# A fused attention and two-layer MoE kernel: the first softmax laid out anew on one Trainium2 core

## The chip, the core and the metric

The kernel runs on one NeuronCore of a Trainium2 chip. The metric is device time in microseconds, here the median of three runs. In the profile PE is TensorE (PEld its weight loads), DVE is VectorE, ACT is ScalarE, POOL is GpSimd, and SP is SyncE, which issues most DMAs.

## The reference, cut to what matters

```python
def mab(q, kv):                       # scale = 1 / sqrt(128)
    s = scale * (q @ kv.T)
    s = s - s.max(-1, keepdims=True)
    a = np.exp(s)
    a /= a.sum(-1, keepdims=True) + 1e-09
    return a @ kv
h = mab(inducing, x)                  # 32 x 128 queries against 12480 tokens: the first softmax
x = mab(x, h)                         # every token against the 32 rows of h: the second softmax
hid = x @ w_in                        # 128 -> 2048
x = (np.maximum(hid, 0) + alpha * np.minimum(hid, 0)) @ w_out     # 2048 -> 128
hid = x @ w_in2
out = (hid * np.cos(hid)) @ w_out2
```

The weights come as 64-bit floats, read as pairs of 32-bit words; the kernel puts fp32 values together from them.

## The kernel before, in words

x is 98 blocks of 128 tokens (the last two of 96). **The first softmax** goes through the blocks in units (UNITS, line 29: 8, 16, 16, 16, 16, 12, 8 and 4 blocks; unit 0 also takes the two short blocks). For a unit, TensorE transposes its blocks four at a time into PSUM (`transposes`, L199), and VectorE (L204) or ScalarE (L206) copies each four to SBUF. TensorE multiplies them with the 32 queries (`u_scores`, L218); VectorE takes the maximum over the unit's columns (L230) and spreads it over a masked tile mm4 (L232); TensorE sums that into the tile tm (`u_max`, L238), from which VectorE takes the running minimum nbias of the negated maxima (L240). ScalarE forms the exponentials with their row sums zpart, and the factor resc between the old and the new maximum (`u_exp`, L246, L250). VectorE turns the exponentials in 32x32 blocks (L248), TensorE multiplies them with x (`u_pv`, L262), and VectorE adds the product to the running sum hun (`u_sum`, L277) and the denominator to zt (`u_z`, L270). In the loop over units (lines 452 to 480) a unit's transposes stand in two halves, with the scores of the unit before, the exponentials of the one before that, and the products of the unit three back between them. mask4 is kept as a copy in PSUM (L189).

Between the unit's parts a planner, `fill` (line 316), puts **decode** steps: of each quarter of w_in and w_out VectorE takes the magnitude (L362), GpSimd clamps it (L370), ScalarE converts the lower word (L367), VectorE shifts (L374) and joins (L378), GpSimd adds (L382). The planner gives an engine's step only while the granted time (GRANTS) lasts. Nothing is reordered afterwards: every engine runs its instructions in the order of the program.

**After the softmax** tz (L498), the normalised ht (L505), then the product of ht with w_in (`w1_product`, L648), so that the second softmax's weights times w1s give the hidden layer. Tokens then go in tiles of 512. For tile T and slice f, L735 is the hidden product h from the tile's softmax weights a4, ScalarE's L758 its rounded high part, VectorE's L766 the low part, and L778 to L780 three products with the split w_out (tile 0 uses one whole-precision product, L776, two passes). Tiles 0, 1, 2 come first, eight slices of each. The second softmax of a chunk of tokens (`soft_exp`, `soft_norm`) ends with y_at (L575), a high part a_hi (L579) and a low part a_lo (L348, called from there), which SP's DMAs place as the tile's a4 (`load_a4`, L640); for tile 2 these are six loads. From about 155 us on the second layer runs along.

Loads: x comes in parts of 8 blocks on SP's queue, two of four blocks first, but blocks 8 to 15 on ScalarE's queue (line 161), and the words of the weights behind them.

## Time and profile before

| | |
|---|---|
| median of 3 runs | 969.64 us (968.85 to 970.51) |
| span of the profiled execution | 967.3 us |
| busy share of the span: PE, DVE, ACT, POOL | 99%, 84%, 84%, 74% |
| shares of the chain that ended last: PE, DVE | 93%, 3% |

The span is the time from the first to the last instruction of one execution; the profile gives no other time for that execution, and a run's time also holds what lies around its span. A row of the timeline gives start, duration, engine, line, operation, output and input; the brackets at its end are the idle time of the engine before it and what ended it.

### The profile page before, as it was taken

Reading aid. Unit: us, or ns where it says so; the run is one execution under the profiler, and the core shown is the slowest. Engines: PE = TensorE matmul, PEld = TensorE weight load, DVE = VectorE, ACT = ScalarE, POOL = GpSimd, SP = SyncE. Lnnn points to the kernel's source line nnn. Section 1 sums busy time; section 2 is a strip of 40 time slices with the busy share of each in tenths; the row PEclk is TensorE's granted clock in tenths of the full one; section 3 lists DMA queues with packets and bytes.
Section 4 is the critical chain, followed back from the end, with each engine's and each line's share of the span. In section 5 each row is a group of like instructions: output and inputs, shape, how many; then the busy total and the mean of one; then the engine's idle time right before and its main releaser. Section 6 shows DMA issues by size and latency. Waiting matters only on the chain.

```text
span 967.3 us, 14953 instructions
## 1 busy us (share of the span) xinstructions
PE 955.3 (99%) x4608; PEld 771.6 (80%) x4608; DVE 810.2 (84%) x1378; ACT 810.8 (84%) x1577; POOL 712.6 (74%) x698
## 2 busy tenths in 40 slices
PE   8899999999999999999999999999999999999998
PEld 5566778888888888888888888888888888888886
DVE  4886877888888888888988888898888888888888
ACT  4677877888888888888888888898888888888897
POOL 2265656477778777877887778788777777877896
PEclk9999999999999999999999999999999999999999
DMA  9320000000000000000000000000000000000000
GB/s 360 147 93 25 25 17 9 1 1 20 19 20 2 12 20 20 1 12 20 20 1 21 11 17 4 20 20 12 1 20 20 2 11 20 20 1 15 12 13 16
DMA packets 12143, 26.54 MB, mean 27 GB/s; under 512 B 2752, under 2 KB 3360, under 8 KB 12064
## 3 DMA queue, kind: packets, MB, share of 16 engines
q1 hardware_dynamic: 11520, 24.95, 7.5%
q8 instruction: 36, 0.59, 0.3%
q10 hardware_dynamic: 544, 0.65, 0.2%
q14 instruction: 43, 0.35, 0.1%
HBM read 14.80 MB, written 6.39 MB: 22 GB/s over the span
## 4 chain that ended last, share of the span: by engine, by line
PE 93%; DVE 3%; ACT 1%; DMA 1%; issue 1%; POOL 0%; SPq 0%; ACTq 0%; DVEq 0%; POOLq 0%
PE h L812 9%; PE h L813 9%; PE h L814 9%; PE yacc L875 9%; PE yacc L873 9%; PE h L735 9%; PE yacc L874 9%; PE xacc L780 8%; PE xacc L779 8%; PE xacc L778 8%; PE xacc L776 1%; PE s L218 1%; DMA xp<-x_main 1%; PE tp L199 1%; PE xacc L786 1%
## 5 line engine op out<-in xcount | busy, mean ns | idle before, releaser
L348 POOL TENSOR_TENSOR lo<-g,hi 128x512 fp32r<-128x512 f32 (+1 forms) x398 | 505.7, 1273 | 160.7 <-PE yacc L874 42.3
L827 DVE SCALAR_TENSOR_TENSOR r<-k,h 128x512 f32<-128x512 int32 (+1 forms) x400 | 268.8, 672 | 103.1 <-ACT k L821 95.2
L821 ACT ACTIVATE k<-h 128x512 int32<-128x512 f32 (+1 forms) x400 | 235.2, 588 | 100.2 <-PE h L814 87.3
L839 DVE SCALAR_TENSOR_TENSOR g<-r,h 128x512 f32<-128x512 f32 (+1 forms) x400 | 266.9, 667 | 3.2 <-ACT r L833 1.7
L766 DVE SCALAR_TENSOR_TENSOR lo<-h,hi 128x512 fp32r<-128x512 f32 (+1 forms) x371 | 246.6, 670 | 21.0 <-ACT hi L758 20.3
L833 ACT ACTIVATE r<-r 128x512 f32<-128x512 f32 (+1 forms) x400 | 246.9, 617 | 1.6 <-DVE r L827 1.6
L758 ACT ACTIVATE hi<-h 128x512 fp32r<-128x512 f32 (+1 forms) x371 | 214.9, 581 | 19.5 <-PE h L735 18.0
L735 PE MATMUL h<-a,w1s 128*128 128x512 f32 (+1 forms) x400 | 158.9, 401 | 1.3 <-DMA a<-a_hi 0.5
L875 PE MATMUL yacc<-lo,wo 128*128 128x512 f32 (+1 forms) x400 | 154.5, 386 | 0.4 <-POOL lo L348 0.4
L873 PE MATMUL yacc<-hi,wo 128*128 128x512 f32 (+1 forms) x400 | 154.6, 386 | 0.0
L874 PE MATMUL yacc<-hi,wo 128*128 128x512 f32 (+1 forms) x400 | 154.0, 385 | 0.0
L780 PE MATMUL xacc<-lo,wp 128*128 128x512 f32 (+1 forms) x384 | 148.2, 386 | 0.0
L779 PE MATMUL xacc<-hi,wp 128*128 128x512 f32 (+1 forms) x371 | 142.8, 385 | 0.0
L778 PE MATMUL xacc<-hi,wp 128*128 128x512 f32 (+1 forms) x371 | 142.4, 384 | 0.0
L859 ACT ACTIVATE hi<-g 128x512 fp32r<-128x512 f32 (+1 forms) x201 | 124.4, 619 | 1.2 <-DVE g L839 1.2
L863 POOL TENSOR_SCALAR hi<-g 128x512 fp32r<-128x512 f32 x189 | 117.5, 622 | 6.0 <-DVE g L839 6.0
L812 PE MATMUL h<-xr_xt,wi 128*128 128x512 f32 (+1 forms) x272 | 105.1, 386 | 0.3
L814 PE MATMUL h<-xr_xt,wi 128*128 128x512 f32 (+1 forms) x272 | 104.2, 383 | 0.0
L813 PE MATMUL h<-xr_xt,wi 128*128 128x512 f32 (+1 forms) x272 | 104.2, 383 | 0.0
L735 PEld LDWEIGHTS h<-a,w1s 128*128 128x128 f32 x400 | 75.2, 188 | 28.4 <-issue 5.4
L875 PEld LDWEIGHTS yacc<-lo,wo 128*128 128x128 f32 x400 | 75.2, 188 | 16.5 <-POOL lo L348 1.3
L873 PEld LDWEIGHTS yacc<-hi,wo 128*128 128x128 f32 x400 | 75.2, 188 | 14.8
(152 smaller groups left out, 1113.4 us busy)
## 6 DMA issues: line engine op xcount, KB each, us to landing
out<-y SPq DMA_DIRECT2D x24, 256.0 KB, 2.0
xp<-x_main SPq DMA_DIRECT2D x10, 512.0 KB, 8.2
raw_wi<-w_in SPq DMA_DIRECT2D x8, 512.0 KB, 9.2
raw_wo<-w_out SPq DMA_DIRECT2D x8, 512.0 KB, 9.0
a<-a_hi SPq DMA_DIRECT2D x40, 64.0 KB, 2.0
a<-a_lo SPq DMA_DIRECT2D x20, 64.0 KB, 2.0
xp<-x_main SPq DMA_DIRECT2D x2, 256.0 KB, 3.5
xp<-x_main ACTq DMA_DIRECT2D x1, 512.0 KB, 7.1
```

Source lines behind the costliest of these rows:

```text
L348: eng.tensor_tensor(out=out, in0=in0, in1=in1, op=ALU.subtract)
L735: mm(t[:, :w], w1s[:, 128 * f:128 * f + 128], a4[T][:, :w], start=True, stop=True)
L766: dve.scalar_tensor_tensor(out=lo[:, :w], in0=t[:, :w], scalar=0.0, in1=hi[:, :w].bitcast(F32), op0=ALU.max, op1=ALU.subtract)
L779: mm(t[:, :w], wslice(wp, f, 1), hi[:, :w], start=False, stop=False)
L780: mm(t[:, :w], wslice(wp, f, 0), lo[:, :w], start=False, stop=False)
L821: act(out=k[:, :w], in_=h2s[T, f][:, :w], func=AF.Copy, bias=0.25)
L827: dve.scalar_tensor_tensor(out=r[:, :w], in0=k[:, :w], scalar=0.25, in1=h2s[T, f][:, :w], op0=ALU.subtract, op1=ALU.subtract)
L833: act(out=r[:, :w], in_=r[:, :w], func=AF.Sin, scale=-TWO_PI)
L839: dve.scalar_tensor_tensor(out=g[:, :w], in0=r[:, :w], scalar=TWO_PI, in1=h2s.pop((T, f))[:, :w], op0=ALU.mult, op1=ALU.mult)
L873: mm(t[:, :w], wslice(wo, f, 0), hi[:, :w], start=(f == 0), stop=False)
L874: mm(t[:, :w], wslice(wo, f, 1), hi[:, :w], start=False, stop=False)
L875: mm(t[:, :w], wslice(wo, f, 0), lo[:, :w], start=False, stop=(f == NF - 1))
```

## The change

1. Units of 8, 16, 16, 16, 16, 16 and 8 blocks: seven instead of eight. 2. All transposes of a unit in one run; nine of the groups of four are copied by VectorE, at other places than before. 3. `u_scores` is cut into products and `u_top` (maximum and mask multiply), `u_exp` into exponentials and `u_turn`; the loop's order is new. 4. Blocks 8 to 15 are loaded on SP's queue. 5. The denominator `u_z` goes to GpSimd. 6. mask4 is read in SBUF. 7. The planner's grants are new. 8. The second w1 product moves from before tile 0 into its steps. 9. `warm` (transposes whose result nobody reads) takes a PSUM tile of its own.

```diff
@@ -26,7 +26,7 @@
-UNITS = [(0, 8), (8, 16), (24, 16), (40, 16), (56, 16), (72, 12), (84, 8), (92, 4)]
+UNITS = [(0, 8), (8, 16), (24, 16), (40, 16), (56, 16), (72, 16), (88, 8)]
@@ -88,9 +88,8 @@
     NU = len(UNITS)
-    PV = 3
...
-    GRANTS = {2: (0.3, 0.1), 3: (0.45, 0.2), 4: (0.45, 0.2), 5: (0.45, 0.2)}
...
+    GRANTS = {3: (0.5, 0.25), 4: (0.5, 0.25), 5: (0.5, 0.25), 6: (0.5, 0.25)}
     ident = const.tile([128, 128], F32, name="ident")
@@ -158,7 +157,7 @@
     nc.scalar.dma_start(out=xp[12][0:96], in_=x_tail)
-    load_x(nc.scalar, 8, 8)
+    load_x(nc.sync, 8, 8)
     nc.scalar.dma_start(out=alph, in_=alpha)
@@ -185,8 +184,6 @@
     tmt = ps_tile("acc", "tm")
-    mask = tmt[:, 504:508]
-    dve.tensor_copy(out=mask, in_=mask4)
     tht, pv_last = tmt[:, 112:240], tmt[:, 240:368]
@@ -199,7 +196,7 @@
-        k = nb // 2 if b0 == 92 else nb if b0 in (0, 8, 24, 40) else 0
+        k = nb if b0 in (0, 12, 20, 28, 36, 48, 64, 80, 92) else 0
         if k:
@@ -207,8 +204,9 @@
+        t = ps_tile("h2", "warm")
         for _ in range(n):
-            nc.tensor.transpose(pvt[1][:, 384:512], ident, ident)
+            nc.tensor.transpose(t[:, 0:128], ident, ident)
@@ -227,9 +225,12 @@
         scores(t, o, indt, b0, nb, 4)
...
+    def u_top(n):
+        t = s1t[n]
         dve.reduce_max(out=mxu[:, n:n + 1], in_=t[:, 0:32 * len(unit_blocks(n))], axis=AX.X)
         mm4 = xpool.tile([128, 4], F32, tag="mm4", name="mm4", bufs=2)
-        dve.tensor_scalar(out=mm4, in0=mask4 if n == NU - 1 else mask, scalar1=mxu[:, n:n + 1], scalar2=None, op0=ALU.mult)
+        dve.tensor_scalar(out=mm4, in0=mask4, scalar1=mxu[:, n:n + 1], scalar2=None, op0=ALU.mult)
         s1t[n, "m"] = mm4
@@ -241,23 +242,26 @@
         w = 32 * len(unit_blocks(n))
-        p = xs[:, 5]
-        pt = ptt[n] = xs[:, n % 5]
+        p = xs[:, 4 + n % 2]
+        pt = ptt[n] = xs[:, n % 4]
         act(out=p[:, :w], in_=s1t.pop(n)[:, :w], func=AF.Exp, scale=scale, bias=nbias[:, n:n + 1],
             accum_out=zpart[:, n:n + 1])
-        dve.transpose(out=pt[:, :w], in_=p[:, :w])
         if n:
             act(out=resc[:, n:n + 1], in_=nbias[:, n - 1:n], func=AF.Exp, scale=-1.0, bias=nbias[:, n:n + 1])
+        s1t[n, "p"] = p
...
+    def u_turn(n):
+        w = 32 * len(unit_blocks(n))
+        dve.transpose(out=ptt[n][:, :w], in_=s1t.pop((n, "p"))[:, :w])
...
-    def u_pv(n, half):
+    def u_pv(n):
         bl = unit_blocks(n)
         r = pv_region(n)
-        h = len(bl) // 2
-        for k in range(h * half, h if half == 0 else len(bl)):
+        for k in range(len(bl)):
             g = k % 4
@@ -265,10 +269,10 @@
         if n == 0:
-            dve.tensor_copy(out=z, in_=zpart[:, 0:1])
+            pool.tensor_copy(out=z, in_=zpart[:, 0:1])
         else:
-            dve.scalar_tensor_tensor(out=z, in0=z, scalar=resc[:, n:n + 1], in1=zpart[:, n:n + 1],
-                                     op0=ALU.mult, op1=ALU.add)
+            pool.tensor_scalar(out=z, in0=z, scalar1=resc[:, n:n + 1], scalar2=zpart[:, n:n + 1],
+                               op0=ALU.mult, op1=ALU.add)
@@ -451,56 +455,51 @@
         b0, nb = UNITS[n]
-        quads = [(b0 + k, 4) for k in range(0, nb, 4)]
         gd, ga = GRANTS.get(n, (0.0, 0.0))
-        for k in quads[:max(1, len(quads) // 2)]:
-            transposes(*k)
+        for k in range(0, nb, 4):
+            transposes(b0 + k, 4)
         if n == 0:
             transposes(96, 2, 96)
+        fill(1.9, dve=gd, act=ga)
+        if n >= 4:
+            u_sum(n - 4)
+        if n >= 2:
+            u_max(n - 2)
         if n >= 1:
...
             u_exp(n - 2)
-        fill(1.8, dve=2 * gd, act=2 * ga)
-        if n >= PV:
-            u_pv(n - PV, 0)
-            u_pv(n - PV, 1)
-        if n == NU - 1:
-            u_scores(n)
-        for k in quads[max(1, len(quads) // 2):]:
-            transposes(*k)
+            u_z(n - 2)
+            u_turn(n - 2)
+        if n >= 3:
+            u_pv(n - 3)
         if n >= 1:
-            u_max(n - 1)
-        if n >= PV:
-            u_z(n - PV)
-            u_sum(n - PV)
+            u_top(n - 1)
         if n == 2:
             dve.tensor_scalar(out=om_a, in0=alph, scalar1=-1.0, scalar2=1.0, op0=ALU.mult, op1=ALU.add)
-        if n < NU - 1:
-            fill(1.8, dve=2 * gd, act=2 * ga)
-    u_pv(NU - 3, 0)
-    u_pv(NU - 3, 1)
+        fill(2.1, dve=gd, act=ga)
+    u_max(NU - 2)
+    u_scores(NU - 1)
+    u_exp(NU - 2)
+    u_z(NU - 2)
+    u_sum(NU - 4)
+    u_pv(NU - 3)
+    u_top(NU - 1)
+    u_turn(NU - 2)
     u_max(NU - 1)
-    u_exp(NU - 2)
     u_exp(NU - 1)
-    warm(3)
-    u_pv(NU - 2, 0)
-    u_pv(NU - 2, 1)
-    u_z(NU - 3)
+    u_z(NU - 1)
+    u_pv(NU - 2)
     u_sum(NU - 3)
-    u_z(NU - 2)
-    warm(2)
-    u_pv(NU - 1, 0)
-    u_pv(NU - 1, 1)
...
-    u_z(NU - 1)
+    u_turn(NU - 1)
     tz = ps_tile("h2", "tz")[:, 0:32]
     mm(tz, zt.to_broadcast([128, 128]), id32, start=True, stop=True)
+    u_pv(NU - 1)
     u_sum(NU - 2)
...
     dve.reciprocal(out=zr, in_=zr)
-    warm(3)
+    warm(2)
     mm(tht, hun, ssum2, start=True, stop=True)
@@ -671,7 +670,6 @@
     run(e1, 1)
-    w1p1 = w1_product(1)
     act(out=w1s[0:96, 0:512], in_=w1p[0:96, :], func=AF.Copy)
@@ -679,9 +677,7 @@
     run(e1, 2)
-    act(out=w1s[0:96, 512:1024], in_=w1p1[0:96, :], func=AF.Copy)
     run(e1, 3, 4)
-    w1_low(1, w1p1)
     plan(("soft", 2), "soft", then(soft_exp(2), soft_norm(2)), first=True)
@@ -928,7 +924,7 @@
         soon = steps[s + 2][0] if s + 2 < S else None
-        if soon and soon[0] == 0 and soon[1] in (8, 12):
+        if soon and soon[0] == 0 and soon[1] in (4, 8, 12):
             w1_parts(soon[1] // 4, w1_product(soon[1] // 4))
```

Where the order moves, as the built programs have it. First **VectorE, one unit in the middle of the softmax**, before (mm is the masked tile, tm holds the sums of maxima, xs the exponentials, s the scores in PSUM, k_t and g_ab decode's steps):

```order
L230 TENSOR_REDUCE mxu<-s_349 128x1
L232 TENSOR_SCALAR mm_355<-tm,mxu 128x4
L248 STREAM_TRANSPOSE xs<-xs 128x512
L240 TENSOR_REDUCE nbias<-tm 128x1
L270 SCALAR_TENSOR_TENSOR zt<-zt,resc,zpart 128x1
L277 SCALAR_TENSOR_TENSOR hun<-hun,resc,pv_161 128x128
L362 TENSOR_SCALAR g_ab<-raw_wi_131 128x512
```

and now:

```order
L279 COPY hun<-pv_160 128x128
L241 TENSOR_REDUCE nbias<-tm 128x1
L255 STREAM_TRANSPOSE xs<-xs 128x512
L231 TENSOR_REDUCE mxu<-s_359 128x1
L233 TENSOR_SCALAR mm_385<-mask_67,mxu 128x4
L378 TENSOR_SCALAR k_t_294<-g_ab 128x512
L201 COPY xt_89<-tp 128x512
L382 SCALAR_TENSOR_TENSOR k_t_294<-raw_wo_123,k_t_294 128x512
```

The turn stood ahead of the minimum nbias and belonged to the unit before; now it stands right behind the minimum, and belongs to the same unit. The denominator step zt has gone to GpSimd; there it stands ahead of decode's clamps and adds:

```order
L274 TENSOR_SCALAR zt<-zt,resc,zpart 128x1
L374 TENSOR_SCALAR g_ab<-g_ab 128x512 x2
L274 TENSOR_SCALAR zt<-zt,resc,zpart 128x1
L386 TENSOR_TENSOR win_86<-k_t_291,win_86 128x512
L274 TENSOR_SCALAR zt<-zt,resc,zpart 128x1
L386 TENSOR_TENSOR wout_87<-k_t_294,wout_87 128x512
```

Before, the same clamps and adds followed each other there with nothing between them. Third, **VectorE from decode to the a_lo of tile 2**, before (wa belongs to the folded weights, sT and rz to the second softmax, h_801 is the first product of tile 1):

```order
L560 RECIPROCAL rz_80<-rz_80 128x8
L571 TENSOR_TENSOR sT<-sT,rz_80 128x256
L696 TENSOR_TENSOR wa<-twt,alph 128x128
L575 STREAM_TRANSPOSE y_at<-sT 128x256
L542 STREAM_TRANSPOSE sT<-s_750 128x512
L545 TENSOR_REDUCE mx_79<-sT 128x16
L766 SCALAR_TENSOR_TENSOR lo_805<-h_801,hi_804 128x512
L348 TENSOR_TENSOR a_lo<-y_at,a_hi 128x256
```

and now (h_767 is the first product of tile 1):

```order
L762 SCALAR_TENSOR_TENSOR lo_771<-h_767,hi_770 128x512
L557 TENSOR_REDUCE rz_80<-sT 128x8
L558 TENSOR_SCALAR rz_80<-rz_80 128x8
L559 RECIPROCAL rz_80<-rz_80 128x8
L570 TENSOR_TENSOR sT<-sT,rz_80 128x256
L762 SCALAR_TENSOR_TENSOR lo_788<-h_784,hi_787 128x512
L574 STREAM_TRANSPOSE y_at<-sT 128x256
L762 SCALAR_TENSOR_TENSOR lo_797<-h_793,hi_796 128x512
L762 SCALAR_TENSOR_TENSOR lo_808<-h_801,hi_807 128x512
L352 TENSOR_TENSOR a_lo<-y_at,a_hi 128x256
```

The denominator, the division and the turn of chunk 2 have moved behind the first low part of tile 1, and a_lo behind the fourth.

## Rows read from the trace of the kernel before

**Rows 1.** Windows by stage: length, busy us of each engine (instructions), PEclk, DMA, GB/s
```profile
15.93:38.70 22.77, 21.31 (x371) 14.97 (x372) 20.10 (x58) 16.57 (x42) 6.27 (x7) 1.00 0.78 307
...
55.40:64.67 9.27, 9.27 (x39) 5.70 (x39) 5.95 (x11) 6.82 (x13) 5.80 (x7) 1.00 0.10 32
64.67:950.00 885.33, 884.13 (x3947) 722.95 (x3947) 753.01 (x1222) 759.76 (x1450) 678.70 (x646) 1.00 0.05 14
```
**Rows 2.** Timeline of TensorE: eight transposes early, products and eight transposes later
```profile
8.90 1.94 PE L199 MATMUL tp<-ident,xp 128*128 128x128 f32 x8 [2.21 <-DMA xp<-x_main]
...
26.86 1.06 PE L262 MATMUL pv<-xp,xs 128*32 128x128 f32 x32
27.85 1.09 PE L199 MATMUL tp<-ident,xp 128*128 128x128 f32 x8
```
**Rows 3.** DMA issues: count, KB each, median us from issue to landing
```profile
xp<-x_main SPq DMA_DIRECT2D x2, 256.0 KB, 3.5
```
**Rows 4.** Timeline of VectorE in one unit of the first softmax
```profile
24.23 0.68 DVE L230 TENSOR_REDUCE mxu<-s 128x1 f32<-128x512 f32 x1
24.95 0.22 DVE L232 TENSOR_SCALAR mm<-tm,mxu 128x4 f32<-128x4 f32 x1
25.08 0.70 DVE L248 STREAM_TRANSPOSE xs<-xs 128x512 f32<-128x512 f32 x1
...
25.88 0.34 DVE L277 SCALAR_TENSOR_TENSOR hun<-hun,resc,pv 128x128 f32<-128x128 f32 x1
26.14 0.42 DVE L362 TENSOR_SCALAR g_ab<-raw_wi 128x512 int32<-128x512 int32 x1
```
**Rows 5.** Timeline: exponential of 512 columns; minimum, exponential and turn of 256 columns
```profile
18.73 0.68 ACT L246 ACTIVATE xs<-s,nbias 128x512 f32<-128x512 f32 x1
...
35.21 0.18 DVE L240 TENSOR_REDUCE nbias<-tm 128x1 f32<-128x28 f32 x1
...
35.48 0.47 ACT L246 ACTIVATE xs<-s,nbias 128x256 f32<-128x256 f32 x1 [0.54 <-DVE nbias L240]
...
36.08 0.45 DVE L248 STREAM_TRANSPOSE xs<-xs 128x256 f32<-128x256 f32 x1
```
**Rows 6.** Timeline of VectorE: a copy of four blocks, decode's shift and join
```profile
14.47 0.69 DVE L204 COPY xt<-tp 128x512 f32<-128x512 f32 x1 [0.39 <-PE tp L199]
...
29.95 0.41 DVE L374 TENSOR_SCALAR k_t<-g_ab 128x512 int32<-128x512 int32 x1
30.40 0.69 DVE L378 SCALAR_TENSOR_TENSOR k_t<-raw_wi,k_t 128x512 int32<-128x512 int32 x1
```
**Rows 7.** Timeline: GpSimd adds, and a small VectorE operation beside one
```profile
24.45 1.27 POOL L382 TENSOR_TENSOR wout<-k_t,wout 128x512 int32<-128x512 int32 x1 [1.15 <-DVE k_t L378]
...
52.37 1.27 POOL L382 TENSOR_TENSOR win<-k_t,win 128x512 int32<-128x512 int32 x1 [0.16 <-DVE k_t L378]
52.59 1.08 DVE L559 TENSOR_SCALAR rz<-rz 128x8 f32<-128x8 f32 x1
```
**Rows 8.** Timeline of VectorE: first low part of tile 1, a_lo of tile 2
```profile
57.13 0.69 DVE L766 SCALAR_TENSOR_TENSOR lo<-h,hi 128x512 fp32r<-128x512 f32 x1 [0.90 <-ACT hi L758]
57.74 0.41 DVE L348 TENSOR_TENSOR a_lo<-y_at,a_hi 128x256 fp32r<-128x256 f32 x1
```
**Rows 9.** Timeline of SP, loads of tile 2: the second and the last; DMA issues
```profile
58.19 0.51 SPq L640 DMA_DIRECT2D a<-a_lo  x1
...
60.65 0.59 SPq L640 DMA_DIRECT2D a<-a_hi  x1
...
a<-a_hi SPq DMA_DIRECT2D x8, 32.0 KB, 1.8
```
**Rows 10.** Chain that ended last: a whole-precision pair, scores of 16 blocks, a split product
```profile
48.95 0.86 PE xacc L776 x2
...
57.96 1.00 PE s L218 x8
...
60.70 0.23 PE xacc L779
```

## The prediction

> **What bounds the kernel now.** I read the busy time by stage first [rows 1]. From 64.67 us (the first product of the third token tile) to 950 us TensorE is busy 884.13 of 885.33 us: nothing else can end anything there, so whatever the change moves before 64.67 us arrives at the end one for one. All of the diff's work lies before it. In the first softmax, 15.93 to 38.70 us, TensorE is busy 21.31 and VectorE 20.10 of 22.77 us: two engines close to full, and the question is which one the new layout makes the longer. From 55.40 to 64.67 us TensorE never idles; what it needs there must be on time.
>
> The profiled span is 967.3 us, the median of the three runs 969.64. I work out a difference on the span and add it to the median; the 2.3 us around the span stay.
>
> **1. Until the first full reduce.** Now TensorE waits 2.21 us for blocks 8 to 15, and the eight transposes after that wait take 1.94 us; at 27.85 eight take 1.09 [rows 2]. The load becomes the third on SP's queue, issued near 2.2 us. The two before it land 3.5 us after issue [rows 3], on ScalarE's queue it lands at 8.8; so 5.7 to 8.8, and I take 7.0. But the scores of unit 0 now stand behind sixteen transposes instead of four, and behind VectorE's third copy and its memset. Forward from 7.0: sixteen transposes 3.9 (at the slow rate; 2.2 at the fast one), last copy and memset 0.8, scores 1.3, sixteen transposes of unit 2 2.1, copy 0.7, and on VectorE the minimum, exponential and turn of unit 0, which now stand ahead of the reduce of unit 1, 1.6: 17.4; with fast transposes and scores 15.0. I take 16.5, nearer the slow end since the slow rate in [rows 2] lasts right up to there. It is 15.93 now [rows 1]: **+0.6** (-0.9 to +1.5).
>
> The Trainium skill (DMA: Bandwidth & Descriptors, section on issuing engines not being separate DMA queues) says that loads from either queue run on the same 16 engines and interleave, so that a second issuing engine saves only issue time. By that rule the move alone brings the load no sooner, and the total would be that of the fourth rival below; no run here shows it yet.
>
> **2. VectorE's chain per unit.** An instruction starts up to 0.1 us before the one ahead of it ends (turn at 25.08, multiply at 24.95 for 0.22). From start to start I take reduce 0.72, multiply 0.13, turn 0.63, sum 0.26, decode's magnitude 0.3 [rows 4], minimum 0.1 [rows 5], a 512-column copy 0.65, shift 0.45, join 0.61 [rows 6]. Now the order in a unit is reduce, multiply, turn of the unit before, minimum: the exponential that the turn needs was started by the previous minimum, and VectorE does not wait. In the new order the minimum of a unit is followed at once by its own turn. Between them stands ScalarE: exponential 0.27 us after the minimum's start, turn 0.60 after that for 256 columns, and 0.21 more for 512 (0.68 against 0.47) [rows 5]. So **1.08 us from a minimum to its turn, of which VectorE works 0.1**, five times, with everything behind it in its queue waiting too. TensorE gets the next products of maxima only after the multiply, and stalls behind them.
>
> To that come nine copies instead of four and a half (+4.5 x 0.65 = 2.9), less the eight denominator steps that go to GpSimd (0.1 each), one unit less (0.9) and 0.4 of decode.
>
> There is one price more. The multiply reads mask4 in SBUF instead of PSUM. An SBUF operation of that size, 128x8, took 1.08 us while a GpSimd add ran beside it, ending as that add ended; the multiply from PSUM took 0.22 at 24.95, inside the add at 24.45 to 25.72 [rows 4, 7]. In the new order the denominator steps stand ahead of decode's GpSimd steps and wait for the exponential, which pushes clamps and adds onto the multiplies of units 2, 3 and 4. I count 0.4, 0.5 and 0.45: 1.35 (0 if they miss one another, 3.0 if each meets an add whole).
>
> Reduce to reduce, with what the order puts between: unit 1 to 2, 0.72 + 0.13 + 0.13 (om_a) + 0.65 + 2 x 0.31 (magnitudes) + 1.08 + 0.63 = 3.96; 2 to 3, with the hold 0.4, shift and join 1.06 and the first sum 0.2, 4.87; 3 to 4, with 0.5, 1.06 and 0.26, 5.03; 4 to 5, with 0.45, 0.3 and 0.26, 4.22; from there to the minimum of the last unit 3.62 (0.85, decode 1.06, 1.08, 0.63); to the last sum about 2.15 (exponential 0.27 and 0.5, resc 0.3, GpSimd's denominator 0.2 and its product 0.3 ahead of the last eight products 0.5). Sum 23.85 us, against 22.77 from the full reduce to the last sum now [rows 1]: **+1.1** (-0.25 without any hold, +2.7 with all). TensorE's own work per 16-block unit is 2.1 transposes, about 0.9 scores and 1.0 products [rows 2, 10] and some 0.2 of maxima, 4.2, less than VectorE's 4.5, so it is not the bound.
>
> **3. Hand-over.** The second w1 product leaves the wait before the first tile and stands in another gap, before the transposes of the second tile's weights: nothing. With its copy and subtraction gone from ahead of that tile's exponential, VectorE is 0.5 us earlier there, but TensorE has the product itself, 0.86. Decode stands behind: wout's second quarter is only begun after the softmax, its scaled copy comes late for the fifth product of the first tile: **+0.2** (0 to +0.9).
>
> **4. Loads of the third tile.** The a_lo split for it now ends at 58.15, and the last of its six loads is issued at 60.65 and lands 1.8 later, 62.45 [rows 8, 9], 2.2 us before TensorE wants it at 64.67. In the new order VectorE has decode, then the third chunk's turn and maximum, then the first low part of tile 1, and only then denominator, division and turn of chunk 2 (0.41 + 0.17 + 0.2 + 0.43 + 0.43 at 256 columns, priced by the 0.41 of [rows 8]), with three more low parts at 0.61 among them, before a_lo: 57.13 + 4 x 0.61 + 1.64 = 61.2, and 0.41 for itself, 61.6. The loads follow as before, 4.3 us: 65.9. TensorE is there sooner: 8 products h and 12 split products at 0.23, 3 whole-precision pairs at 0.86, one set of scores 1.0 [rows 10] make 8.2 after 55.40, so 63.6. **+2.2 us** of idle TensorE, nothing behind it can pass (0 if the loads overlap better than now, +3.1 with one GpSimd hold).
>
> Equal units, one run of transposes and "three units late" by themselves cost nothing: the products already are three units late.
>
> **Sum**: 0.6 + 1.1 + 0.2 + 2.2 = 4.1: span 971.4, median **973.7 us**, +0.4%. A measurement of this kernel tells about 0.2% (1.94 us) from no change.
>
> **The rivals.**
> - *The loads are in time*: only the softmax term is left, 969.64 + 1.9 = 971.5. For: DMA issues could come earlier than VectorE's queue lets me think. Against: from the second issue to the last it takes 2.46 us in [rows 9], and a_lo is in front. Chance 0.17.
> - *TensorE slows down*: it would idle 1 to 2 us at several units and 2.2 at the loads. The transposes after the wait of 2.21 us run at half the later rate [rows 2], though the granted clock column reads 1.00 (2.4 GHz) for the stages of [rows 1]. Half rate for the last two units' products costs 1.5, after the loads 1 or more: 976.2. Against: the transposes before that wait were slow as well. The Trainium skill (TensorE: Matmul & The Clock Gate, part 1) states that an idle array falls to 1.2 GHz and activity brings back 2.4; by that rule this rival holds if the waits are long enough. Chance 0.12.
> - *TensorE, not VectorE, carries the softmax*, and it ends earlier. If VectorE's wait for the exponential were filled, a unit costs 4.2 and the stage ends with TensorE's own work: 72 transposes 9.2, scores 5.4, products 6.1, maxima 1.2 from the memset at 11.7, 33.6, and 2 of tail, 35.6 instead of 38.70. With terms 3 and 4 that is 968.9, no slower than before; with the loads in time 966.7, faster. It decides where VectorE's unit falls under 4.2. For: TensorE never waits for x. Against: the order puts turn right behind minimum. Chance 0.12.
> - *Blocks 8 to 15 still land at 8.8*: term 1 grows by 1.8, 975.5. For: all x loads share the traffic of the first 20 us, and this one gains only its place in a line. Against: the line ahead of it is two loads of 256 KB. Chance 0.06.
> - Something else, such as waits further on by a shifted order of decode, about no change: 0.04. The forecast keeps 0.49.
>
> **How the numbers follow.** Slower by over 0.2% (above 971.6) are nearly all of the forecast, the slow TensorE, the late blocks, and little of the first rival; faster (below 967.7) half of the third and a part of the unknown: 0.12 faster, 0.24 same, 0.64 slower. The range goes from the third rival's 968.9 to the second's 976.2; the forecast's own is 971.6 to 975.6.
>
> **What would show it.** Right: in the changed profile every turn of a unit has idle VectorE before it, ended by the exponential, about 1 us; TensorE waits for the mask multiply; the last sum starts near 40.4; a wait of TensorE of some 2 us for a_hi near 65. Wrong: no idle before the turns and a last sum before 38 (third rival); no DMA wait near 65 (first); transposes or products past 30 us at half rate (second).

## The result, and the profile after

The changed kernel takes **982.28 us** (median of four runs, 981.52 to 982.78) against 969.44 (968.85 to 970.51) for the kernel before, run beside it: ratio 1.0126, 95% interval 1.0114 to 1.0138. It is slower by 12.8 us. 973.7 had been predicted, in a range up to 976.2: the sign was right, the size three times too small.

Where the time went is read from windows whose edges are the same events in every kernel: start of the full reduce of unit 1, start of the last sum, and the starts of the first product h of tile 1, of tile 2, of tile 3 and of tile 8. First the profile after (columns as in [rows 1]):

```profile
0.00:18.26 18.26, 13.38 (x90) 10.18 (x91) 5.53 (x14) 5.35 (x10) 4.34 (x17) 0.81 0.90 336
18.26:41.96 23.70, 18.10 (x338) 12.45 (x336) 18.32 (x46) 12.38 (x32) 6.32 (x11) 1.00 0.67 257
41.96:48.62 6.66, 4.57 (x40) 2.95 (x40) 5.08 (x17) 2.75 (x8) 1.79 (x2) 1.00 0.01 2
48.62:60.13 11.51, 10.79 (x48) 5.14 (x49) 8.45 (x19) 8.64 (x19) 6.04 (x7) 1.00 0.19 51
60.13:71.87 11.74, 8.89 (x34) 4.81 (x35) 8.92 (x16) 7.74 (x15) 6.71 (x7) 1.00 0.21 65
71.87:113.00 41.13, 39.35 (x187) 25.96 (x188) 27.04 (x46) 30.74 (x60) 21.11 (x21) 1.00 0.14 43
113.00:201.37 88.37, 84.94 (x366) 66.83 (x367) 66.98 (x104) 66.09 (x120) 48.97 (x50) 0.98 0.04 11
```

The same windows of the kernel before, beside the two that stand in [rows 1]:

```profile
0.00:15.93 15.93, 11.65 (x74) 8.08 (x75) 3.86 (x11) 4.91 (x9) 4.13 (x16) 1.00 0.89 330
...
38.70:45.20 6.50, 5.66 (x46) 3.72 (x46) 5.04 (x17) 2.77 (x8) 1.13 (x2) 1.00 0.01 3
45.20:55.40 10.20, 9.47 (x46) 4.82 (x47) 9.32 (x22) 8.15 (x19) 5.66 (x6) 1.00 0.29 93
...
64.67:103.74 39.07, 38.59 (x186) 25.38 (x185) 30.06 (x50) 30.86 (x63) 21.05 (x22) 1.00 0.16 48
103.74:188.09 84.35, 83.73 (x367) 65.76 (x368) 65.53 (x104) 65.82 (x119) 49.47 (x51) 1.00 0.05 12
```

In lengths, with two kernels of the experiments (runs e10 and e9 below):

| stage | before | after | softmax of after, order of before | softmax of before, order of after |
|---|---|---|---|---|
| to the full reduce | 15.93 | 18.26 | 17.05 | 15.42 |
| to the last sum | 22.77 | 23.70 | 24.76 | 22.48 |
| to the first h | 6.50 | 6.66 | 6.44 | 6.50 |
| first half of tile 0 | 10.20 | 11.51 | 10.22 | 11.51 |
| first half of tile 1 | 9.27 | 11.74 | 9.25 | 11.73 |
| tile 2 to tile 3 | 39.07 | 41.13 | 39.54 | 42.76 |
| tile 3 to tile 8 | 84.35 | 88.37 | 84.41 | 88.20 |

After minus before: 2.33 + 0.93 + 0.16 = 3.42 up to the first h, then 1.31 + 2.47 + 2.06 + 4.02 = 9.86, of which the prediction had only term 4 and the 0.2 of term 3. The distance is 13.28 us at the start of tile 8 and 13.25 at the last product. These are single executions; how far the first row varies is said under term 1.

What TensorE waited for from 45 to 200 us (engine and line, releaser, us in total, times, longest), before:

```profile
PE tst L619 <- DVE y_st L348: 0.7, 1, 0.7
PE h L735 <- DMA a<-a_hi: 0.5, 1, 0.5
PE h L735 <- DVE lo L766: 0.4, 2, 0.2
```

and after:

```profile
PE h L731 <- DVE lo L762: 4.0, 5, 2.5
PE h L731 <- DMA a<-a_hi: 4.0, 2, 2.6
PE tst L618 <- DVE y_st L352: 1.4, 1, 1.4
PE xacc L772 <- ACT w1t L412: 0.4, 1, 0.4
```

The wait of 2.6 for a_hi is the one that term 4 priced. The longest for a low part, 2.5, lies in tile 6, nearly 130 us after the softmax. VectorE there, after:

```profile
164.09 0.69 DVE L800 TENSOR_TENSOR xr_xt<-xacc,xr_xt 128x512 fp32r<-128x512 f32 x1 [0.23 <-ACT xr_xt L799]
164.70 0.68 DVE L557 TENSOR_REDUCE rz<-sT 128x16 f32<-128x512 f32 x1
165.41 1.24 DVE L558 TENSOR_SCALAR rz<-rz 128x16 f32<-128x16 f32 x1
166.68 0.25 DVE L559 RECIPROCAL rz<-rz 128x16 f32<-128x16 f32 x1
166.85 0.67 DVE L378 TENSOR_SCALAR dec<-g_ab 128x512 int32<-128x512 int32 x1
167.56 0.69 DVE L382 SCALAR_TENSOR_TENSOR k_t<-raw_wo,dec 128x512 int32<-128x512 int32 x1
168.17 1.88 DVE L762 SCALAR_TENSOR_TENSOR lo<-h,hi 128x512 fp32r<-128x512 f32 x3
```

and TensorE (the last h before the stop; then the h after it, the first of six split products, and the next h):

```profile
165.98 0.39 PE L731 MATMUL h<-a,w1s 128*128 128x512 f32 x1
168.91 0.71 PE L731 MATMUL h<-a,w1s 128*128 128x512 f32 x1 [2.54 <-DVE lo L762]
169.41 0.63 PE L774 MATMUL xacc<-hi1p,wp 128*128 128x512 f32 x1
...
171.97 0.61 PE L731 MATMUL h<-a,w1s 128*128 128x512 f32 x1
```

The planner has put the denominator of a later chunk (reduce, +1e-9, reciprocal) and two steps of the backlog of decode right behind one another, with the +1e-9 held for 1.24; for 4.3 us no low part is made. After the idle 2.54 us the seven products from 168.91 to 171.97 come 0.43 apart and not 0.23 as in [rows 10]: 1.5 us more. The granted clock is 0.52 from 168.90 to 172.00 us: nearly all of that stretch ran at the lower level of 1.2 GHz. The stop costs 4.0 in all.

In the softmax, VectorE in one unit after:

```profile
25.18 0.16 DVE L241 TENSOR_REDUCE nbias<-tm 128x1 f32<-128x12 f32 x1
26.25 0.71 DVE L255 STREAM_TRANSPOSE xs<-xs 128x512 f32<-128x512 f32 x1 [0.91 <-ACT xs L247]
26.89 0.65 DVE L231 TENSOR_REDUCE mxu<-s 128x1 f32<-128x512 f32 x1
27.58 0.60 DVE L233 TENSOR_SCALAR mm<-mask,mxu 128x4 f32<-128x4 f32 x1
```

Minimum to turn is 1.07 (forecast 1.08), with 0.91 idle, and the mask product is held (0.60, against 0.22 in [rows 4]). At the start, against the first line of [rows 2]:

```profile
8.00 3.23 PE L196 MATMUL tp<-ident,xp 128*128 128x128 f32 x16 [2.25 <-DMA xp<-x_main]
12.19 1.29 PE L216 MATMUL s<-xt,indt 128*32 128x64 f32 x14 [0.96 <-DVE s L225]
13.41 2.93 PE L196 MATMUL tp<-ident,xp 128*128 128x128 f32 x16
```

### The profile page after: what moved, and what is told of

Read it like the earlier page. It is cut to its first block, busy times and chain, and to the rows that moved or that the text cites. A ratio compares the mean times of both kernels' runs of the same rounds, so it can differ in the third digit from the quotient of the medians.

```text
span 981.0 us, 14901 instructions
## 1 busy us (share of the span) xinstructions
PE 955.6 (97%) x4586; PEld 771.0 (79%) x4586; DVE 811.0 (83%) x1368; ACT 808.9 (82%) x1569; POOL 715.6 (73%) x705
## 4 chain that ended last, share of the span: by engine, by line
PE 89%; DVE 2%; issue 1%; ACT 1%; POOL 1%; SPq 1%; DMA 0%; POOLq 0%; DVEq 0%; ACTq 0%
PE h L808 9%; PE h L809 9%; PE h L810 9%; PE yacc L871 9%; PE yacc L869 9%; PE yacc L870 9%; PE h L731 9%; PE xacc L776 8%; PE xacc L775 8%; PE xacc L774 8%; PE xacc L772 1%; DVE lo L762 1%; SPq L639 1%; PE xacc L782 1%; POOL lo L352 1%
```

## The experiments

Two theories stood against each other. **Order**: the 9.9 us behind the softmax come from the order in which the planner now issues decode, denominators and low parts, since the softmax leaves another backlog and the second w1 product has moved. **Inherited**: they follow from the later start alone. Ratios are to the kernel before on the same chip; "us" is the ratio's distance from 1 times 969.4, which makes the change 12.2.

### One part at a time, and the backlog

**e1**, the second w1 product back:

```
     run(e1, 1)
+    w1p1 = w1_product(1)
...
+    act(out=w1s[0:96, 512:1024], in_=w1p1[0:96, :], func=AF.Copy)
     run(e1, 3, 4)
+    w1_low(1, w1p1)
-        if soon and soon[0] == 0 and soon[1] in (4, 8, 12):
+        if soon and soon[0] == 0 and soon[1] in (8, 12):
```

> The changed kernel with one part undone: the second w1 product, its copy and its low part stand ahead of the first tile again. Changed kernel: 982.3; of its 13.3 us, 3.4 are there at the first h product, and some 10 come later (2.6 a wait for the third tile's load near 70 us, 4.2 a stop near 169 us). Theory 'order' (the late part comes from the order in which the planner now issues the steps between the products): with the product moved back the denominators of chunk 2 stand ahead of tile 1's low parts again, so the wait of 2.6 for a_hi near 70 goes; 978 to 980, and less if the stop near 169 goes with it. Rival 'inherited' (the later start alone makes the late part: everything is shifted against the loads): nothing but the place of 0.9 us of TensorE changes, 981.5 to 983.

977.06, ratio 1.0072 (1.0060 to 1.0083), 7.0 us, just below the expected range. The wait for a_hi is down to 0.5, the stop of 2.5 in tile 6 stays, and a wait of 1.98 for y_st has come into tile 0. From the first h to tile 12 its profile takes 327.61 us, against 330.74 in the changed kernel and 320.91 before. A step moved in the hand-over changes a wait 25 us later: order.

**e2**, more decode in the softmax:

```
-    GRANTS = {3: (0.5, 0.25), 4: (0.5, 0.25), 5: (0.5, 0.25), 6: (0.5, 0.25)}
+    GRANTS = {2: (0.4, 0.2), 3: (0.9, 0.4), 4: (0.9, 0.4), 5: (0.9, 0.4), 6: (0.9, 0.4)}
```

> The changed kernel with larger grants, so that the second quarter of wout is decoded within the softmax too, a little more than in the kernel before. Theory 'order': the waits for a_hi near 70 and the stop near 169 both go (the last decode steps come earlier among the low parts, after 59 and 69 of them and not 67 and 73), for some 1 us more of VectorE in the softmax: 975 to 978. Rival 'inherited': the late part stays, the softmax gets longer: 982.5 to 984.

976.04, 1.0051 (1.0039 to 1.0063). The first h is at 51.57, 3 us later still, and yet the total is 7 us less: from the first h to tile 12 it takes 321.21 us, against 330.74 in the changed kernel and 320.91 before. Waits for low parts are 1.3 in all, none for a_hi. "Inherited" is out: the latest start has a late part as short as that of the kernel before.

**e3**, the turn later:

```
             u_z(n - 2)
-            u_turn(n - 2)
         if n >= 3:
             u_pv(n - 3)
         if n >= 1:
             u_top(n - 1)
+        if n >= 2:
+            u_turn(n - 2)
```

> The changed kernel with one line in another place: a unit's turn stands behind the next unit's maximum and mask product on VectorE, not straight behind its own minimum. Term 2 of the prediction (VectorE is the bound and waits some 0.9 us for each of five exponentials): those waits go, the first h product is 3 to 4 us earlier, at 45 to 45.8 and not 48.6, and the total falls by about that much, 978 to 979.5, if the later stops stay as they are. Rival (TensorE or the loads carry the softmax, the waits of VectorE are slack): first h product stays at 48 to 48.6, total 981.5 to 982.5.

977.77, 1.0072 (1.0059 to 1.0085). Its softmax:

```profile
17.41:38.28 20.87, 18.65 (x344) 13.09 (x343) 18.26 (x45) 13.15 (x34) 7.01 (x12) 1.00 0.79 310
```

20.87 and not 23.70, 1.9 under the kernel before, first h at 44.94; TensorE works without a wait from 17.3 to 31.8. The late part is untouched (330.83 from first h to tile 12). So term 2 was the turn's place, and this layout without that wait, and with a decode step less, is what the third rival described.

**e4**, the other way round: the kernel before with a backlog.

```
-    GRANTS = {2: (0.3, 0.1), 3: (0.45, 0.2), 4: (0.45, 0.2), 5: (0.45, 0.2)}
+    GRANTS = {2: (0.3, 0.1), 3: (0.2, 0.1), 4: (0.2, 0.1), 5: (0.2, 0.1)}
```

> The kernel before with smaller grants alone: its softmax leaves the same decode steps undone that the changed kernel leaves (second quarter of wout untouched), all else as before. Theory 'order': the softmax itself is no longer, the first h product is not later than 45.2, yet waits turn up among the first eight tiles, and the total is 2 to 6 us above the kernel before, 971.5 to 975.5. Rival 'inherited': without a later start there is no late part: 968.5 to 970.

974.05, 1.0033 (1.0021 to 1.0045), 3.2 us, with waits for low parts of 2.1, for a_hi of 1.2 and for w1t of 0.9; from the first h to tile 12 it is 3.6 longer than before. The grants of three units have changed, and nothing in the layout of the softmax. Its first h came at 46.61, which the expectation had excluded: blocks 8 to 15 were there at 9.63 us in this profile, 0.7 later than before.

**e5**, blocks 8 to 15 on ScalarE's queue again, the rest as changed:

```
-    load_x(nc.sync, 8, 8)
+    load_x(nc.scalar, 8, 8)
```

> The changed kernel with blocks 8 to 15 loaded from ScalarE's queue again, all else as in the changed kernel. In five profiles so far the first of these blocks was there at 7 to 8 us from SP's queue and at 8.9 and 9.9 from ScalarE's. Theory 'the queue brings the load earlier': the sixteen transposes start at 8.9 or later, the first h product is 0.9 to 1.9 us later than 48.6, total 983 to 984.3. Rival (the page's rule in the prediction: either queue runs on the same engines, the place of issue gives nothing): start at 8.0, total as the changed kernel, 981.8 to 982.8.

982.79, 1.0138 (1.0124 to 1.0152): no difference to the changed kernel that these intervals tell apart, though in the profile the blocks are there at 9.62 and not 8.00. The later load is largely made up by faster transposes (the second sixteen take 2.00 and not 2.93). On the total nothing speaks against the rule that the prediction cited (the Trainium skill, DMA: Bandwidth & Descriptors, issuing engines are not separate DMA queues). The landing itself is another matter: 6.9 to 8.0 in the ten profiles from SP's queue where TensorE waited for it, 8.6 to 9.6 in four from ScalarE's (the 9.9 in the expectation is 9.63 in e4's profile).

**e6**, transposes of the identity in the wait:

```
+        if n == 1:
+            warm(14)
         for k in range(0, nb, 4):
             transposes(b0 + k, 4)
```

> The changed kernel with fourteen transposes of the identity (some 1.9 us of TensorE) put into its wait for blocks 8 to 15, so that it does not stand idle there. In the profile of the changed kernel the granted clock is 0.5 from 8.6 to 15.3 us after that wait. Theory 'the wait costs the clock': the clock stays 1.0, the sixteen transposes and the sixteen after them take 2.2 each and not 3.2 and 2.9, the full reduce starts 1.5 to 2 us earlier than 18.3 and the first h product about as much earlier, 46.6 to 47.2; total 980.3 to 981. Rival (that stretch waits for loads and copies, not for the clock): the full reduce moves by less than 0.4, total 981.8 to 982.8.

979.83, 1.0103 (1.0088 to 1.0119), some 2 us under the changed kernel, with intervals that hardly overlap. The start in its profile:

```profile
7.33 1.04 PE L196 MATMUL tp<-ident,xp 128*128 128x128 f32 x8
8.63 1.07 PE L196 MATMUL tp<-ident,xp 128*128 128x128 f32 x8 [0.26 <-ACT xt L203]
10.66 0.74 PE L216 MATMUL s<-xt,indt 128*32 128x64 f32 x14 [0.96 <-DVE s L225]
11.34 2.00 PE L196 MATMUL tp<-ident,xp 128*128 128x128 f32 x16
```

All at the fast rate; the full reduce starts at 15.26 and not 18.26. That filling the wait did this is likely but not shown: e1 and e7 put nothing into it, waited 1.39 and 1.53 us there, and ran the same transposes just as fast (1.06, 1.06 and 2.00; the full reduce at 15.41 in e1). The total speaks for it.

**e7**, e3's edit and larger grants:

```
-    GRANTS = {3: (0.5, 0.25), 4: (0.5, 0.25), 5: (0.5, 0.25), 6: (0.5, 0.25)}
+    GRANTS = {2: (0.4, 0.2), 3: (0.7, 0.3), 4: (0.7, 0.3), 5: (0.7, 0.3), 6: (0.4, 0.2)}
```

> The turn behind the next unit's mask product, and larger grants, so that the second quarter of wout is decoded in the softmax as in the kernel before. If the softmax term and the order term are two separate causes, both go: first h product near 45 to 47 (one or two more decode steps on VectorE), no wait over 1 us for a_hi or for a low part from 46 to 200 us, total 969 to 972. If they are not separate (more decode in the softmax costs again what the turn won, as the 3 us by which grants alone made it longer), 973 to 976.

970.80, 1.0022 (1.0010 to 1.0033). First h at 44.94, waits for low parts of 0.6 at most, none for a_hi: both causes gone, and 10 of the 12 us with them. Its times scatter: seven of the eleven lie from 969.7 to 971.2, four from 973.7 to 974.3, and the profile is of one of the seven.

**e8**, the mask read from PSUM:

```
+    mask = tmt[:, 504:508]
+    dve.tensor_copy(out=mask, in_=mask4)
...
-        dve.tensor_scalar(out=mm4, in0=mask4, scalar1=mxu[:, n:n + 1], scalar2=None, op0=ALU.mult)
+        dve.tensor_scalar(out=mm4, in0=mask4 if n == NU - 1 else mask, scalar1=mxu[:, n:n + 1], scalar2=None, op0=ALU.mult)
```

> The changed kernel with the mask copied into PSUM and read from there again. Prediction: the mask product is held beside a GpSimd add when it reads SBUF; three of seven took 0.60 to 0.66 and not 0.23. Theory: they take 0.22 again, the softmax is 1.0 to 1.3 us shorter, total 981 to 981.4. Rival (the hold has to do with GpSimd, not with where the operand lies, or the time is given back at the turn, which waits for the exponential anyway): total 981.8 to 982.8.

981.39, 1.0124 (1.0110 to 1.0138): no measurable difference. The product is no longer held:

```profile
25.75 0.22 DVE L235 TENSOR_SCALAR mm<-tm,mxu 128x4 f32<-128x4 f32 x1
30.38 0.22 DVE L235 TENSOR_SCALAR mm<-tm,mxu 128x4 f32<-128x4 f32 x1
```

and from the full reduce to that of the last unit it gains 0.57 (19.09 against 19.66). But in this execution TensorE's waits of 1.60 and 2.03 near 30 and 34 us are followed by a granted clock of 0.50 from 36 to 38, where thirty-two products take 2.01 and not 1.06, and the stage ends no shorter (23.80).

### Softmax and order apart

**e9** and **e10** exchange the two halves. Behind the softmax each runs the other kernel's order on every engine, to the last instruction. e9 is the kernel before with e4's grants, no decode step in its softmax that the changed kernel leaves undone there, the second w1 product late, and (shown) the planner set to the changed kernel's state; e10 is the changed kernel with e1's edit, grants of (0.5, 0.25) for units 2 to 6, and the state of the kernel before.

```
...
+    now[0], pool_free[0] = 28.0, 26.62
+    spare.update(act=0.43, dve=-0.237, pe=0.0)
+    for chain in [c for c in queue if c[0] == ("in", 1)]:
+        chain[3][:5] = (24.85, 26.62, 26.87, 28.785, 29.052)
     u_pv(NU - 3, 0)
...
```

> The softmax of the kernel before, and from its end on the order of the changed kernel on every engine: the same decode steps are left undone, the planner's clock and balances are set to what they are there in the changed kernel, and the second w1 product stands late. Theory 'two separate costs' (softmax 3.4 us, order some 9 to 10, which add up): first h product at about 45, and the waits near 70, 105 and 169 us as in the changed kernel: 977 to 980. Rival (the order costs only because the softmax ended later, against loads that come when they come): 969.5 to 972.

> The softmax of the changed kernel, and from its end on the order of the kernel before on every engine, the second w1 product in its old place included; within the softmax the first two decode steps of the second quarter of wout come back, some 1.4 us of VectorE and ScalarE at most. Two separate costs: no stop over 1 us from 46 to 200 us, first h product at 48 to 50 and the same distance kept to the end: 972.5 to 975. Rival as for the run above: waits return, 976 to 980.

e9: 978.51, 1.0089 (1.0074 to 1.0103), **8.6 us for the order alone**. e10: 973.13, 1.0037 (1.0025 to 1.0049), **3.6 us for the softmax alone**, with no stop over 1 us behind it. 8.6 + 3.6 = 12.2, the whole; each of the two is known to within 1.4 and 1.2 us, and e10's softmax holds decode steps that the changed kernel's leaves undone, so that the sum comes out so exactly is luck. The table above has their stages: behind the first h they are those of the kernel whose order they took over, within 0.02 us up to tile 2 and within 0.2 from tile 3 to tile 8; only the stage between differs, by 0.5 and 1.6 (in e9 the products after the wait for a_hi come 0.45 apart, at a granted clock of 0.50).

The time from the first h to tile 12 sorts all profiles in the same way. It is 320.9 to 322.0 us in the seven whose softmax begins the second quarter of wout (before, e2, e7, e10 to e12, e15), with the first h anywhere from 42.98 to 51.57. It is 329.6 to 332.2 in the eight that leave it and have the second w1 product late (the changed kernel, e3, e5, e6, e8, e9, e13, e14), with the first h from 44.40 to 49.17. e4 and e1 leave it and have the product early: 324.5 and 327.6. So a late product costs next to nothing where decode is further on (e2, e7), and some 3 us where it is not (e1 against the changed kernel): it is the backlog that costs. On VectorE that backlog is a single step left undone in the softmax, the magnitude (L366) of that quarter: nine decode steps there, and not the ten of the kernel before.

**e11** is e10 with the turn later, **e12** is e11 with the scores of unit 0 and their maximum ahead of unit 1's transposes:

```
         if n == 0:
             transposes(96, 2, 96)
+            u_scores(0)
+            u_top(0)
...
-        if n >= 1:
+        if n >= 2:
             u_scores(n - 1)
...
-        if n >= 1:
+        if n >= 2:
             u_top(n - 1)
```

> As the run above, with each turn behind the next unit's mask product. Theory (the turn's place is the whole of term 2): the softmax is shorter than in the kernel before by 0 to 2 us, as from full reduce to first h product it took 27.5 with the turn later, 29.3 in the kernel before and 30.4 in the changed one, and now has two more decode steps: total 967.5 to 970. Rival (with those decode steps VectorE is the bound again): 970.5 to 973.

972.14, 1.0022 (1.0011 to 1.0032). 1.5 better than e10, short of what was expected. The softmax takes 22.73 and not 24.76, but e3 had 20.87: VectorE has 47 instructions there and not 45, and is busy 19.43 us and not 18.26, since more of decode is back.

> As the run above, and the scores of unit 0 with their maximum stand ahead of the transposes of blocks 8 to 23 and not behind them. Term 1 of the prediction put the delay of the full reduce on those scores behind sixteen transposes, on the memset behind the copies (0.96 of waiting), and on slow transposes. If the first two count, TensorE does the scores within its wait for the load: 2 us or so less, 965.5 to 968. If the start is set by the load and what follows it alone: no difference to the run above within 0.7.

970.44, 1.0007 (0.9999 to 1.0016): 1.4 better again, level with the kernel before; the 2 us expected were too many.

**e13 to e15** ask whether VectorE is the bound that is left. e13 takes three copies off it in the changed kernel, e14 puts the denominator back on it (the two `pool.` calls of u_z become `dve.`, the second as scalar_tensor_tensor), e15 is e12 with e13's copies and e8's mask.

```
-        k = nb if b0 in (0, 12, 20, 28, 36, 48, 64, 80, 92) else 0
+        k = nb if b0 in (0, 12, 20, 36, 64, 80) else 0
```

> The changed kernel with six of its quads copied by VectorE and not nine (blocks 28, 48 and 92 go to ScalarE). Theory (term 2: VectorE's chain of a unit is the softmax's bound, and a copy of 0.65 in it counts in full): from full reduce to last sum 22 to 22.5 and not 23.7, total 980.3 to 981. Rival (the turn's wait for the exponential swallows it, since the minimum and the exponential come no earlier): 23.4 to 23.8, total 981.6 to 982.6.

982.85, 1.0126 (1.0112 to 1.0140), as the changed kernel. Its profile shows the shorter stage that the theory wanted (22.48), but the profiled execution was the fastest of the four, 980.82, and the other three took 982.7 to 983.9. In the profile 1.4 is given back behind the wait of 2.56 for a_hi, where seven products come 0.44 apart at a granted clock of 0.50. What the other three lose no trace shows: open.

> The changed kernel with the steps of the denominator on VectorE again. Prediction (0.1 us each, and on GpSimd they push the clamps and adds onto the mask products): VectorE does eight steps of 0.1 more, each waits for the second exponential, 0.3 us ahead of each turn, and the holds of the mask product change place: within 1.2 us of the changed kernel to either side, 981.2 to 983.5. If GpSimd's denominators were the cause of a large part of the softmax's 3.4 us: 979 to 980.5.

984.51, 1.0140 (1.0123 to 1.0157), if anything more than the changed kernel, and above the expected range: the denominators on GpSimd are not what costs.

> Turn later, first scores early, old order behind the softmax, six copies on VectorE, mask in PSUM. If VectorE was the bound of the run with the first scores early (there from full reduce to last sum 22.7): 1.5 to 2 us less, 968 to 969, under the kernel before by some 1 us. If TensorE or the loads bound it: 969.5 to 970.5, as without.

968.31 against 970.42 beside it, **0.9981 (0.9972 to 0.9990)**: faster than both kernels. From full reduce to last sum:

```profile
15.39:36.52 21.13, 17.79 (x336) 12.36 (x336) 17.77 (x45) 15.24 (x38) 8.73 (x14) 1.00 0.86 346
```

In e12 VectorE was busy 19.42 of 22.71; with the three copies and the held products off it, it is busy 17.77 and the stage is 1.58 shorter, so VectorE was the bound there.

## Why the prediction was wrong, step by step

**The step that failed** is the first reading: "From 64.67 us ... TensorE is busy 884.13 of 885.33 us: nothing else can end anything there, so whatever the change moves before 64.67 us arrives at the end one for one." The windows of [rows 1] show that for the order that the kernel before happens to have. The planner behind the softmax keeps what it has and has not emitted, its clock and its balances, and the change hands it another state; so the steps of VectorE from 45 to 170 us stand in another order, and waits appear in tiles 0 to 6 that no row of before could show. Past the start of the third tile, where this reading put nothing, lie 2.06 + 4.02 = 6.08 us: two thirds of the 9.2 by which the sum of 4.1 fell short of the 13.3 in the profile. e9 prices the whole order, with what terms 3 and 4 had foreseen of it, at 8.6 us; e4 reaches 3.2 with nothing changed but the grants. The prediction named the mechanism among its leftovers ("waits further on by a shifted order of decode, about no change: 0.04"): the price was wrong, not only the chance.

**Term 4** (+2.2, loads of the third tile) is one of these waits, read from the order of both kernels, and it was right: 11.74 against 9.27, +2.47 (its own figures, 65.9 against 63.6, make 2.3). The same reading was needed up to tile 8; there lay 2.06 (with a wait of 1.46 for the loads of tile 3) and 4.02 (the stop in tile 6).

**Term 1** (+0.6, bound +1.5) came out at +2.33 in the one profile of the changed kernel. The blocks were there at 8.00, not 7.0, and the sixteen transposes after the scores took 2.93, not 2.1. But this part varies from run to run more than the term: e1 has the same order up to there, its blocks were there at 7.08, all its transposes went at the fast rate, and its full reduce started at 15.41, earlier than before. The 16.5 taken lies between the two executions, so +2.33 does not show the term to be wrong. In e10, with two decode steps ahead of that reduce, it was +1.1.

**Term 2** (+1.1) was right in its mechanism, and closer in its sum than its parts were: 23.70 from full reduce to last sum, 23.85 forecast, but 21.03 to the minimum of the last unit (21.70 forecast) and 2.67 behind it (2.15 forecast, where the listed parts add up to 2.07). The minimum-to-turn step was 1.07, 1.08 forecast, with VectorE idle ahead of six of the seven turns, 0.85 to 0.91 us ahead of four; GpSimd's hold of the mask product three times 0.37 to 0.43, 1.17 in place of 1.35. e3 shows that the turn's place makes it, and e8 that the holds make little of it.

**Term 3** (+0.2, bound +0.9) was too small: 0.16 in the hand-over, and 1.31 in the first half of tile 0. "Stands in another gap ...: nothing" for the second w1 product held for TensorE's own time (what its place does to the order further on is e1's matter). Before, TensorE waited 0.73 ahead of the transposes of the second tile's weights (L619, now L618); now the product stands ahead of them and the wait is gone. From the first h to these transposes it is 2.87 us before and 2.84 after (TensorE before, then after):

```profile
48.07 0.64 PE L619 MATMUL tst<-ident,y_st 128*96 128x128 f32 x4 [0.73 <-DVE y_st L348]
```

```profile
49.92 1.02 PE L647 MATMUL w1p<-win,ht 128*128 128x512 f32 x2
...
51.46 0.60 PE L618 MATMUL tst<-ident,y_st 128*96 128x128 f32 x4
...
58.69 1.13 PE L772 MATMUL xacc<-hi_f,w1t 128*128 128x512 f32 x2 [0.41 <-ACT w1t L412]
60.13 0.47 PE L731 MATMUL h<-a,w1s 128*128 128x512 f32 x1 [0.32 <-ACT hi_f L739]
```

and on ScalarE:

```profile
58.23 1.28 ACT L412 ACTIVATE w1t<-wout,om_a 128x128 f32<-128x128 f32 x4 [1.38 <-POOL wout L386]
59.42 0.57 ACT L739 ACTIVATE hi_f<-h 128x512 f32<-128x512 f32 x1
```

The loss is the late w1t that the term named, for the fifth product: 0.6 there, and 0.8 more because ScalarE's 1.28 us of w1t then hold up the hi_f for which the next h waits. With the second quarter of wout decoded earlier and the product just as late, the first half of tile 0 takes 10.42 (e2) and 10.43 (e7), against 11.51 here and 10.20 before.

**The rivals.** Slow TensorE came twice, though not in the last units of the changed kernel: at the start, where the granted clock is 0.50 from 9 to 15 us after the wait of 2.25, and after the stop in tile 6. The Trainium skill (TensorE: Matmul & The Clock Gate, part 1) has an idle array fall to 1.2 GHz; the trace agrees in these two places, but after the equally long wait of 2.56 for a_hi the next products come 0.24 apart and the granted clock stays at 1.00. TensorE did not carry the softmax, because of the turn; in e3 it does. Blocks 8 to 15 gained 0.9 us in this profile, between the 1.8 taken and the nothing of the fourth rival.

## What to carry to other kernels

Where a planner with a memory orders the work, an edit upstream is also an edit to every later decision: before calling a saturated stretch safe, compare the order on each engine through all of it, and look for places where several optional steps now stand in a row ahead of something that TensorE waits for. To price a layout by itself, hand the planner the state that it had before; here the two halves then added up. And a turn that follows its own minimum across another engine wants a unit's distance: one line, worth 5 us in the changed kernel (e3) and 1.5 where more decode stands in the softmax (e11).

## What the runs showed of the hardware

- A wait of some 2 us can cost TensorE more behind it than its own length, and does not always. Nine profiles have the stop in tile 6 and eight the long wait for a_hi, 2.53 to 2.73 us each. After eleven of these seventeen waits the next seven products came 0.28 to 0.45 apart, with a granted clock of 0.50 to 0.74 in the 3 us behind the wait; after the other six they came 0.24 to 0.25 apart, with 1.00. In e8 thirty-two products took twice their time after waits of 1.60 and 2.03; the changed kernel has waits of 1.68 and 1.73 at the same places, and there they took 1.06 and 1.08.
- The column of the granted clock does not show every slow stretch: in e10 sixteen transposes from 7.07 on took 3.75 and not 2.00, with 1.00 in the column.
- In the changed kernel a VectorE product of 128x4 with its operands in SBUF took 0.60 to 0.66 when a GpSimd operation was running, ending 0.02 to 0.03 after it, and 0.23 otherwise. With one operand in PSUM it took 0.22 in the middle of a GpSimd add from 25.06 to 26.33 (e8). It agrees with the Trainium skill (SBUF — State Buffer, section on who interferes with whom), by which these two engines lock one another out of a shared pair of ports.
